# Weight loads on a second issuing engine and a planner that books DMA bandwidth, in an attention and MLP kernel

## The chip, the cores and the metric

The kernel runs on one core of a Trainium2 chip. The metric is the device time of one execution in microseconds (us). Before the change the median of three runs was 182.66 us (180.52 to 183.31). Each run carries a state: "slow" where it took over 1.5% more than the fastest run of the same kernel, "fast" otherwise.

The core has five instruction streams that matter here: TensorE (PE, matrix products), VectorE (DVE), ScalarE (ACT), GpSimd (POOL) and SyncE (SP), which only issues DMA transfers. The profile counts the transfers of all streams on the same 16 DMA engines.

## The reference, cut to what matters

```python
def reference(A_x, A_wqkv, A_wo, B_x, B_w1, B_b1, B_w2, B_b2, c, w_mod):   # x 2048 x 448, F = 1792
    mod = (_silu(c) @ w_mod).reshape(1, 6, 1, -1)
    sa, ca, ga, sb, cb, gb = (mod[:, i] for i in range(6))
    h = _layernorm(x) * (1 + ca) + sa
    x = x + ga * attention(h, wqkv, wo)          # 16 heads of 28, window of 8 keys at stride 2
    h = _layernorm(x) * (1 + cb) + sb
    x = x + gb * mlp(h, w1, b1, w2, b2)          # layernorm, w1, gelu, w2
```

## The kernel before

The kernel does not fix the order of its instructions by hand. Every instruction is a *task* with an engine, an estimated duration and its data. A list scheduler, the planner, simulates the engines. At each moment it gives a free engine the ready task of the highest rank. It repeats this 300 times with noise on the ranks and keeps the best plan (the shortest, with a penalty for gaps in PE's work). The plan fixes only the *order on each engine*. On the chip, an engine waits for data, never for the plan's clock. So if a transfer lands later than the plan assumed, everything behind its first user on that engine waits too.

```python
for e in ("PE", "DVE", "ACT", "POOL", "SP"):
    ...
    for t in ready[e]:
        if ready_at[t] > now or (shared and t.port):
            continue
        key = (t.rank + (SAME if e == "PE" and t.mode_in == mode else 0.0), -t.n)
        ...                                   # the task of the highest key starts now
```

All loads but that of the small vector c are issued from SyncE. Each is one task that is as long as its bytes take at 330 GB/s, so that the plan cannot put two loads at the same time:

```python
def load(fn, nbytes, writes, reads=(), bufs=(), free=False):
    t = add("SP", max(0.5, nbytes / DMA_RATE), fn, writes=writes, reads=reads, bufs=bufs, late=1.8,
            order_after=list(chain_dma))
...
load_k(lambda: wqk_st.t[:, 0], A_wqkv[:, 0:D + HP - DH], "wq", [wqk_st])        # four pieces of Wq and Wk
load_k(lambda: wqk_st.t[:, 1], A_wqkv[:, D:2 * D + HP - DH], "wk", [wqk_st])
...                                                                             # x, Wv, wmod, wo
for kt in range(KT):                                                            # w1: 4 pieces of 448 KB
    load(lambda kt=kt: nc.sync.dma_start(out=w1_s[:, kt], in_=B_w1[KOFF[kt]:KOFF[kt] + 128]), F * 256, [f"w1{kt}"], free=True)
for i in range(4):                                                              # w2: 3 of 448 KB, 1 of 224 KB
    ...
```

Five kinds of small transfer lie on the way from one stage to the next, and they use the same SyncE queue:

```python
add("SP", 1.35, lambda b=b: nc.sync.dma_start_transpose(out=hc.t[...], in_=zs[b].t[:]), ..., late=2.2)     # hT <- z
nc.sync.dma_start(out=v_hbm[r0:r0 + 256]..., in_=vs.t[:]...)                    # v_hbm <- vstage, then
nc.sync.dma_start(out=vb.t[...], in_=src(k0s[0], 2))                            # vb <- v_hbm: keys regrouped
nc.sync.dma_start(out=mod_bc[:], in_=mod_hbm[:]....partition_broadcast(128))    # mod_bc: modulation rows to all partitions
nc.sync.dma_start_transpose(out=yT.t[...], in_=y.t[:])                          # yT <- y, the MLP's input
```

In the order of time the kernel copies Wqk into its packed form on VectorE. It multiplies (`pq`, `pv`), does the attention (`lt`, `pd`, `po`), the output product (`pw`) and the MLP (`p<-yT,w_s`, then `p<-w_s,hm`). All these stages overlap for different blocks of rows. The tile `w_s` in the profile is w1 or w2; z and y are outputs of the layernorms, hT and yT the same transposed, rs_all the reciprocal deviations of the layernorms, oT the output of the attention. The matmul `ptr` transposes z at the start, and `pb` multiplies by wmod. A *gate* below is a small GpSimd task that waits for the Wqk copies.

The softmax here doesn't subtract the row's maximum and nothing guards it: scores larger than these inputs give would overflow.

Of the kernel before, what the change touches and what calls it, by code (L numbers as in the profile page):

```python
# [11 lines left out]
FP32 = mybir.dt.float32  # L12
BF16 = mybir.dt.bfloat16
ACT = mybir.ActivationFunctionType
# [6 lines left out]
HP = 32  # L21
FT = F // 128
# [25 lines left out]
DMA_RATE = 330e3  # L48
SWITCH, SAME = 0.095, 1.0
SEM = 0.07  # L50
DRAIN = {"PE": 0.165, "DVE": 0.085, "ACT": 0.105, "POOL": 0.05, "SP": 0.0}
# [27 lines left out]
class Planner:  # L79
# [68 lines left out]
    def forward(self):  # L148
# [13 lines left out]
        while len(order) < len(self.tasks):  # L162
            started = False
            for e in ("PE", "DVE", "ACT", "POOL", "SP"):
# [115 lines left out]
def kernel(  # L280
# [57 lines left out]
    mod_col = cst.tile([128, 2 * KT], FP32, name="mod_col")  # L338
    mod_half = cst.tile([128, 2 * KT], FP32, name="mod_half")
# [29 lines left out]
    chain_dma = []  # L369

    def load(fn, nbytes, writes, reads=(), bufs=(), free=False):
        t = add("SP", max(0.5, nbytes / DMA_RATE), fn, writes=writes, reads=reads, bufs=bufs, late=1.8,
                order_after=list(chain_dma))
        if not free:
            chain_dma[:] = [t]

    def load_k(dst, src, key, bufs=(), free=False):
        n = src.shape[1]
        for h in range(2):
            load(lambda h=h: nc.sync.dma_start(out=dst()[:, 2 * h:2 * h + 2],  # L380
                                               in_=src[KOFF[2 * h]:KOFF[2 * h] + 256].rearrange("(kt p) n -> p kt n", p=128)),
                 256 * n * 2, [key + "ab"[h]], bufs=bufs, free=free)

    def load_m(dst, col, key, bufs, free=False):
        src = w_mod[:, col:col + 2 * D]
        load(lambda: nc.sync.dma_start(out=dst()[:, 0:2], in_=src[0:256].rearrange("(kt p) n -> p kt n", p=128)),
             512 * D * 2, [key + "a"], bufs=bufs, free=free)
        load(lambda: nc.sync.dma_start(out=dst()[:, 3], in_=src[320:448]), 256 * D * 2, [key + "b"], bufs=bufs, free=free)
        load(lambda: nc.sync.dma_start(out=dst()[64:128, 2], in_=src[256:320]), 128 * D * 2, [key + "c"], bufs=bufs, free=free)

    def fill_m(dst, key, bufs, one, rank):

        def fn():
            nc.gpsimd.memset(dst()[0:64, 2], 0.0)
            if one is not None:
                nc.gpsimd.memset(dst()[0:1, 2, one:one + D], 1.0)

        add("POOL", 1.3, fn, writes=[key + "z"], bufs=bufs, rank_add=rank)

    def load_x(b0, b1):  # L400
        load(lambda: nc.sync.dma_start(out=x_all[:, b0:b1, :], in_=xv[b0 // 8, :, b0 % 8:(b1 - 1) % 8 + 1, :]),
             (b1 - b0) * 128 * D * 2, [f"x{b}" for b in range(b0, b1)], free=b0 >= 8)
# [6 lines left out]
    load_x(0, 2)  # L409
    fill_m(lambda: wm_st.t[:], "wm", [wm_st], D, 850)  # L410
    load_m(lambda: wm_st.t[:], 0, "wm", [wm_st])
    load_k(lambda: wqk_st.t[:, 0], A_wqkv[:, 0:D + HP - DH], "wq", [wqk_st])
    load_k(lambda: wqk_st.t[:, 1], A_wqkv[:, D:2 * D + HP - DH], "wk", [wqk_st])
    load_x(2, 4)
    load_k(lambda: Wv[:], A_wqkv[:, 2 * D:3 * D], "wv")
    load_x(4, 8)
# [7 lines left out]
    load(v_pads, 3 * LEAD * DP * 2, ["v_pads"], reads=["warm_w"], free=True)  # L424
    for i in range(2):
        fill_m(lambda i=i: wmod2[i].t[:], f"wmod2{i}", [wmod2[i]], 0 if i == 1 else None, 300)
        load_m(lambda i=i: wmod2[i].t[:], (2 + 2 * i) * D, f"wmod2{i}", [wmod2[i]], free=True)
    add("POOL", 1.6, lambda: nc.gpsimd.memset(wo_s[:], 0.0), writes=["wo"], rank_add=440)
    wo_v = A_wo.rearrange("(ft r d) n -> r d ft n", r=4, d=DH)
    for r in range(4):  # L430
        load(lambda r=r: nc.sync.dma_start(out=wo_s[HP * r:HP * r + DH, :, :], in_=wo_v[r]), D * D // 2, [f"wo{r}"],
             reads=["wo"], free=True)
    for b in (8, 12):
        load_x(b, b + 4)
    b2_bc = sb("zh", [128, D], BF16, "b2_bc")
    load(lambda: nc.sync.dma_start(out=b2_bc.t[:], in_=B_b2.partition_broadcast(128)), 128 * D * 2, ["b2"], bufs=[b2_bc], free=True)
    load(lambda: nc.sync.dma_start(out=b1_rows[:], in_=B_b1.rearrange("(f p) -> f p", p=128)), F * 2, ["b1_rows"], free=True)
    for kt in range(KT):
        load(lambda kt=kt: nc.sync.dma_start(out=w1_s[:, kt], in_=B_w1[KOFF[kt]:KOFF[kt] + 128]), F * 256, [f"w1{kt}"], free=True)
    for i in range(4):  # L440
        f0, f1 = 4 * i, min(4 * i + 4, FT)
        load(lambda f0=f0, f1=f1: nc.sync.dma_start(
            out=w2_s[:, f0:f1], in_=B_w2[128 * f0:128 * f1].rearrange("(ft p) n -> p ft n", p=128)),
            (f1 - f0) * 256 * D, [f"w2l{f // 2}" for f in range(f0, f1, 2)], free=True)
# [10 lines left out]
    def pool_late():  # L455
        gate = add("POOL", 0.1, lambda: nc.gpsimd.memset(wqk_st.t[0:1, :, KT - 1, 0:8], 0.0), bufs=[wqk_st],
                   writes=["wqb", "wkb"])
        for us, fn, writes, reads, ra in late_pool:
# [6 lines left out]
         ["ident"], gated=False, rank_add=800)  # L465
    pool(0.1, lambda: nc.gpsimd.memset(neg_half[:], -0.5), ["neg_half"])
# [72 lines left out]
    def c_cols():  # L539
        for kt in range(KT):  # L540
            nc.tensor.matmul(psc.t[:, kt:kt + 1], lhsT=c_row[0:1, KOFF[kt]:KOFF[kt] + 128], rhs=one1[:],
                             start=True, stop=True)

    P.wrote(add("PE", 0.2, c_cols, mode="32x128", reads=["c_row", "one1"], bufs=[psc]), psc)
    add("ACT", 0.15, lambda: nc.scalar.activation(out=e_c[:], in_=psc.t[:], func=ACT.Exp, scale=-1.0), bufs=[psc],
        writes=["e_c"], after=[tbl0])
    add("DVE", 0.08, lambda: nc.vector.tensor_copy(out=c_col[:], in_=psc.t[:]), bufs=[psc], writes=["c_col"])
    add("DVE", 0.08, lambda: nc.vector.tensor_scalar_add(out=e_c[:], in0=e_c[:], scalar1=1.0), writes=["e_c"])
    add("DVE", 0.1, lambda: nc.vector.reciprocal(out=e_c[:], in_=e_c[:]), writes=["e_c"])

    def silu():
        nc.vector.tensor_tensor(out=silu_bf[:], in0=e_c[:], in1=c_col[:], op=ALU.mult)
        nc.vector.memset(silu_bf[0:64, 2:3], 0.0)
        nc.vector.memset(silu_bf[0:1, 2:3], 1.0)

    add("DVE", 0.2, silu, reads=["e_c", "c_col"], writes=["silu"])
    pscol = ps_one([128, 2 * KT], "ps_col")

    psmod = ps_one([128, 2 * KT], "ps_mod")

    def mod_cols(dst, kts):
        for v in range(2):
            for j in range(KT):
                for kt in kts:
                    nc.tensor.matmul(dst.t[:, v * KT + j:v * KT + j + 1],
                                     lhsT=wm_st.t[:, kt, v * D + KOFF[j]:v * D + KOFF[j] + 128],
                                     rhs=silu_bf[:, kt:kt + 1], start=(kt == kts[0]), stop=(kt == kts[1]))

    P.wrote(add("PE", 0.5, lambda: mod_cols(pscol, (0, 1)), reads=["silu", "wma"], bufs=[pscol, wm_st]), pscol)
    P.wrote(add("PE", 0.5, lambda: mod_cols(psmod, (3, 2)), reads=["silu", "wmb", "wmc", "wmz"], bufs=[psmod, wm_st]), psmod)  # L570
    add("DVE", 0.08, lambda: nc.vector.tensor_copy(out=mod_half[:], in_=pscol.t[:]), bufs=[pscol], writes=["mod_half"], rank_add=50)
    add("DVE", 0.08, lambda: nc.vector.tensor_tensor(out=mod_col[:], in0=psmod.t[:], in1=mod_half[:], op=ALU.add), bufs=[psmod],
        reads=["mod_half"], writes=["sa", "ca"], rank_add=50)
# [467 lines left out]
```

## Time and profile before

| | before |
|---|---|
| median of three runs | 182.66 us |
| span of the profiled run, granted clock of PE | 182.6 us, 0.981 |
| first projection matmul (`pq`) | 11.83 us |
| first MLP matmul (`p<-yT,w_s`) | 73.62 us |
| from there to the end | 109.0 us |

The profiled run took 184.35 us and is marked slow, about 1% above the median.

The first view cuts the span of the kernel before into stretches. The columns are the stretch (start:end) and its length, then the busy time and number of instructions of PE, PEld (weight load), DVE, ACT and POOL, then the granted clock of PE, the busy share of the DMA engines, and GB/s. Two rows are left out.

```profile
6.00:12.00 6.00, 4.86 (x50) 3.15 (x52) 4.04 (x13) 1.02 (x2) 0.99 (x9) 1.00 1.06 342
12.00:20.00 8.00, 7.54 (x120) 4.56 (x119) 4.85 (x17) 6.05 (x19) 2.39 (x13) 1.00 1.05 281
28.00:36.00 8.00, 7.79 (x185) 3.82 (x186) 4.50 (x14) 7.30 (x15) 1.02 (x1) 1.00 0.48 107
36.00:44.00 8.00, 6.15 (x128) 2.92 (x129) 5.05 (x11) 5.20 (x11) 0.00 (x0) 1.00 0.74 155
44.00:52.00 8.00, 7.90 (x166) 3.68 (x152) 7.09 (x22) 6.84 (x13) 1.41 (x3) 1.00 0.79 231
60.00:68.00 8.00, 7.25 (x104) 3.13 (x105) 6.03 (x19) 7.66 (x16) 2.27 (x4) 1.00 1.02 260
68.00:76.00 8.00, 4.62 (x89) 2.06 (x88) 7.97 (x12) 3.62 (x5) 5.82 (x5) 0.77 0.66 134
76.00:84.00 8.00, 8.00 (x34) 2.84 (x34) 4.83 (x18) 4.59 (x8) 3.16 (x5) 0.80 0.00 1
```

Read the PE column: PE is nearly full from 12 us on, so the kernel is bound by PE work. There are two exceptions. From 36 to 44 us PE works 6.15 of 8 us, and 1.7 us of the rest is a wait for the load of vb. From 68 to 76 us PE works 4.62 of 8 us, and the clock drops behind that hole.

The timeline of the kernel before shows what lies where. Its columns are start, duration, engine (SPq is SyncE's queue of issues), line, operation, output<-input, and the count. In brackets is the idle time before it and what ended that.

```profile
9.79 1.42 DVE L675 COPY Wqk<-wqk_st 128x1024 bf16<-128x1024 bf16 x4
11.83 0.82 PE L585 MATMUL pq<-hT,Wqk 128*128 128x256 bf16 x6
44.47 0.57 SPq L439 DMA_DIRECT2D w_s<-in_B_w_dram  x1
45.56 3.65 SPq L439 DMA_DIRECT2D w_s<-in_B_w_dram  x2
55.91 0.82 SPq L442 DMA_DIRECT2D w_s<-in_B_w_dram  x1
59.13 1.99 SPq L442 DMA_DIRECT2D w_s<-in_B_w_dram  x3
68.21 3.44 SPq L903 DMA_TRANSPOSE yT<-y  x2
```

All four Wqk copies are done in a row at 9.8 us, and `pq` starts right after. The MLP weights leave from 44.5 to 61 us. One transpose of y (54.6 us) leaves among them, and the next three leave behind them, from 63.2 us on.

### The profile page before, as it was taken

The page shows a single profiled execution, that of the slowest core. Times are in us where ns is not written, and L with a number is a line of the kernel's source. Part 1 is how long each engine was busy: PE and PEld are TensorE (multiplying, and loading weights), DVE is VectorE, ACT ScalarE, POOL GpSimd, SP SyncE. Part 2 cuts the span into 40 slices and gives each one's busy share as a digit, 9 for nine tenths or more (in the row PEclk, how much of TensorE's full clock was granted, in tenths as well). Part 3 has the DMA queues.
Part 4 walks back from the last instruction along what each step waited for, and adds up shares of the span by engine and source line. Part 5 has one row for each costly group of instructions (what it writes and reads, how often), then busy time and mean ns, then how long its engine had stood idle before and what let it go on. Part 6 is the DMA issues. An engine that isn't in the chain of part 4 may idle for free.

```text
span 182.6 us, 5017 instructions
## 1 busy us (share of the span) xinstructions
PE 169.1 (93%) x2067; PEld 81.0 (44%) x2085; DVE 115.5 (63%) x318; ACT 107.5 (59%) x195; POOL 49.9 (27%) x83
## 2 busy tenths in 40 slices
PE   7799999959999984899999999999999999999993
PEld 2446654424444532233455534455543344443562
DVE  2577795665999969939634738995569974000121
ACT  3237978876885987147574994762893550644300
POOL 8342022001025608726204005336034533000000
PEclk9999999999999999589999999999999999999999
DMA  5999844595779997300220420025110114001011
GB/s 166 330 342 291 240 122 110 129 176 118 197 258 252 259 233 130 96 0 2 61 57 4 140 79 4 0 57 83 34 50 4 31 29 108 0 4 50 0 50 50
DMA packets 28725, 19.84 MB, mean 109 GB/s; under 512 B 14465, under 2 KB 28062, under 8 KB 28702
## 3 DMA queue, kind: packets, MB, share of 16 engines
q1 hardware_dynamic: 28700, 19.52, 40.8%
q8 instruction: 16, 0.26, 0.7%
q14 instruction: 7, 0.06, 0.1%
q10 hardware_dynamic: 2, 0.00, 0.0%
HBM read 12.41 MB, written 3.96 MB: 90 GB/s over the span
## 4 chain that ended last, share of the span: by engine, by line
PE 82%; DMA 8%; ACT 3%; issue 2%; SPq 2%; DVE 1%; ACTq 0%
PE p L950 24%; PE p L585 22%; PE pq L585 9%; PE pw L877 6%; PE p L591 5%; PE pv L585 5%; DMA wm_st<-in_w_mod_dram 3%; PE lt L796 2%; DMA vb<-v_hbm 2%; PE pq L591 2%; DMA yT<-y 2%; PE po L836 2%; PE pwm L498 1%; PE pv L591 1%; PE pd L828 1%
## 5 line engine op out<-in xcount | busy, mean ns | idle before, releaser
L937 ACT ACTIVATE hm<-p,b_col 128x512 bf16<-128x512 f32 x56 | 35.1, 687 | 32.6 <-PE p L585 17.0
L950 PE MATMUL p<-w_s,hm 128*128 128x448 bf16 (+1 forms) x238 | 44.8, 342 | 0.0
L585 PE MATMUL p<-yT,w_s 128*128 128x512 bf16 x160 | 40.7, 394 | 4.1 <-issue 3.9
L523 POOL TENSOR_TENSOR rs_all<-tv_all,neg_half 128x1 f32<-128x1 f32 (+1 forms) x34 | 22.7, 675 | 59.0 <-DVE tv_all L520 53.4
L950 PEld LDWEIGHTS <-hm 128*128 128x128 bf16 x238 | 22.4, 98 | 18.9 <-issue 0.9
L958 DVE TENSOR_TENSOR x_all<-p,x1p 128x448 bf16<-128x448 f32 (+1 forms) x17 | 10.1, 595 | 29.8 <-PE p L950 29.8
L907 POOL TENSOR_TENSOR x1p<-x_all,gbb_bc 128x448 f32<-128x448 bf16 x16 | 17.6, 1108 | 34.2 <-DVE x_all L958 13.3
L585 PEld LDWEIGHTS <-w_s 128*128 128x128 bf16 x168 | 15.6, 100 | 25.5 <-issue 10.6
L585 PE MATMUL pq<-hT,Wqk 128*128 128x512 bf16 (+1 forms) x111 | 22.9, 334 | 0.9 <-issue 0.6
L806 ACT ACTIVATE et<-lt 128x464 bf16<-128x464 f32 x36 | 17.3, 577 | 8.3 <-PE lt L796 8.2
L505 DVE BATCH_NORM_STATS2 st_all<-x_all 128x6 f32<-128x448 bf16 x32 | 18.9, 612 | 2.5 <-DMA x_all<-in_A_x_dram 2.5
L528 DVE TENSOR_SCALAR z<-x_all,mv,rs_all 128x512 bf16<-128x512 bf16 (+1 forms) x32 | 12.2, 403 | 5.8 <-ACT rs_all L514 3.2
L881 DVE TENSOR_TENSOR x_all<-pw,x_all 128x448 bf16<-128x448 f32 x16 | 9.8, 615 | 9.2 <-PE pw L877 9.2
L814 DVE TENSOR_TENSOR et<-et,mask 128x928 bf16<-128x928 bf16 x18 | 11.6, 665 | 6.1 <-ACT et L806 6.1
L877 PE MATMUL pw<-wo_s,oT 128*128 128x448 bf16 x64 | 14.5, 354 | 0.6 <-DVE oT L862 0.5
L585 PEld LDWEIGHTS <-Wqk 128*128 128x128 bf16 x120 | 10.5, 98 | 9.7 <-issue 2.5
L701 ACT CAST qT<-pq 128x512 bf16<-128x512 f32 (+1 forms) x20 | 9.4, 514 | 6.0 <-PE pq L591 3.9
L862 DVE TENSOR_TENSOR oT<-po,den 128x456 bf16<-128x456 f32 x18 | 10.7, 625 | 2.8 <-ACT den L852 2.8
L701 ACT CAST kT<-pq 128x512 bf16<-128x512 f32 (+1 forms) x20 | 9.0, 515 | 3.2 <-PE pq L585 2.3
L585 PE MATMUL pv<-Wv,hT 128*128 128x448 bf16 x48 | 10.4, 353 | 0.0
L715 ACT CAST vstage<-pv 128x448 bf16<-128x448 f32 x16 | 7.9, 561 | 4.1 <-PE pv L591 3.8
L591 PE MATMUL p<-yT,w_s 64*128 64x512 bf16 x56 | 10.3, 401 | 0.0
(85 smaller groups left out, 172.8 us busy)
## 6 DMA issues: line engine op xcount, KB each, us to landing
w_s<-in_B_w_dram SPq DMA_DIRECT2D x7, 448.0 KB, 4.1
vb<-v_hbm SPq DMA_DIRECT2D x18, 128.0 KB, 2.7
v_hbm<-vstage SPq DMA_DIRECT2D x8, 256.0 KB
out_dram<-x_all SPq DMA_DIRECT2D x7, 224.0 KB, 2.9
x_all<-in_A_x_dram SPq DMA_DIRECT2D x3, 448.0 KB, 5.8
wqk_st<-in_A_wqkv_dram SPq DMA_DIRECT2D x4, 226.0 KB
wmod<-in_w_mod_dram SPq DMA_DIRECT2D x2, 448.0 KB
x_all<-in_A_x_dram SPq DMA_DIRECT2D x2, 224.0 KB
```

The source lines that it names most:

```text
L505: add("DVE", 0.53, lambda: nc.vector.bn_stats(out=st_all[:, sl, :], in_=src()), reads=key, writes=[f"st{sl}"])
L523: lambda: nc.gpsimd.tensor_tensor(out=rs_all[:, which, b0:b0 + n], in0=tv_all[:, which, b0:b0 + n], in1=neg_half[:, 0:n], op=ALU.pow),
L528: return add("DVE", us, lambda: nc.vector.tensor_scalar(out=dst(), in0=src(), scalar1=mv[:, b, 0:1], scalar2=rs_all[:, which, b:b + 1], op ...
L585: nc.tensor.matmul(outs[i].t[:], lhsT=w(i, kt, slice(0, 128)), rhs=x(i, kt, slice(0, 128)), start=(n == 0 and not last), stop=(n == 2 and ...
L591: nc.tensor.matmul(outs[i].t[:], lhsT=w(i, kt, rows), rhs=x(i, kt, rows), start=not last, stop=last, tile_position=(r0, 0))
L701: add("ACT", 0.06 + n / 1200, lambda dst=dst, p=pq[i]: nc.scalar.copy(out=dst, in_=p.t[:]), bufs=[pq[i]], writes=w)
L806: ex = add("ACT", 0.45, lambda r=r: nc.scalar.activation(out=et.t[:, r].rearrange("p n ft c -> p (n ft c)"), in_=lts[r].t[:].rearrange("p ...
L814: nc.vector.tensor_tensor(out=ev, in0=ev, in1=mask[:], op=ALU.mult)
L877: nc.tensor.matmul(pw.t[:], lhsT=oT[:, ft, c0:c0 + 128], rhs=wo_s[:, ft, :], start=(ft == 0), stop=(ft == 3))
L907: P.wrote(add("POOL", 1.05, lambda: nc.gpsimd.tensor_tensor(out=xp.t[:], in0=x_all[:, t, :], in1=gbb2_bc[:], op=ALU.add), reads=[f"x{t}", ...
L937: gl = add("ACT", 0.57, lambda f=f, p=p1[i]: nc.scalar.activation(out=hm_at(f), in_=p.t[:], func=ACT.Gelu_apprx_tanh, bias=b1_col[:, f:f + ...
L950: nc.tensor.matmul(p2.t[:], lhsT=hm_at(f)[:, bi * 128:(bi + 1) * 128], rhs=w2_s[:, f, c0:c1], start=(f == 0), stop=(f == FT - 1))
```

## The change

The intent was to let the weights leave from another engine, so that they no longer stand in SyncE's queue ahead of small urgent transfers. The planner was also to know that bandwidth is shared. Three things were done.

1. Nineteen bulk loads (wmod, wo, x blocks 8 to 15, b2, w1, w2) are issued from GpSimd, each ordered behind the one before it in the plan ("one piece in flight"). That is an ordering edge in the plan, not a wait on the chip.
2. The planner has a sixth engine, BW. Each transfer is a short issue task and a task on BW of its bytes at 340 GB/s. A DMA transpose is booked as 400 KB.
3. The modulation weights are loaded as 4 chunks of 112 rows in place of 128-row pieces, which needs no zero fill.

```diff
-DMA_RATE = 330e3
+DMA_RATE, TR_BYTES = 340e3, 400e3
-            for e in ("PE", "DVE", "ACT", "POOL", "SP"):
+            for e in ("PE", "DVE", "ACT", "POOL", "SP", "BW"):
...
+    def dma(eng, issue, fn, nbytes, writes=(), reads=(), bufs=(), order_after=(), late=1.8, rank_add=0.0):
+        t = add(eng, issue, fn, reads=reads, bufs=bufs, order_after=order_after, rank_add=rank_add, port=None)
+        u = add("BW", nbytes / DMA_RATE, lambda: None, writes=writes, bufs=bufs, order_after=[t], late=late)
+        return t, u
+
+    def head(fn, nbytes, writes, reads=(), bufs=()):
+        t, u = dma("SP", 0.5, fn, nbytes, writes, reads, bufs, list(chain["head"]))
+        chain["head"] = [t]
+
+    def bulk(fn, nbytes, writes, reads=(), bufs=()):
+        t, u = dma("POOL", 0.8, fn, nbytes, writes, reads, bufs, chain["head"] + chain["bulk"], 2.2)
+        chain["bulk"] = [t] + chain["bulkbw"][-1:]
+        chain["bulkbw"].append(u)
...
-        load(lambda kt=kt: nc.sync.dma_start(out=w1_s[:, kt], in_=...), F * 256, [f"w1{kt}"], free=True)
+        bulk(lambda kt=kt: nc.gpsimd.dma_start(out=w1_s[:, kt], in_=...), F * 256, [f"w1{kt}"])
...
-            add("SP", 1.35, lambda b=b: nc.sync.dma_start_transpose(out=hc.t[...], in_=zs[b].t[:]),
-                bufs=[hc, zs[b]], writes=[(hc, "raw", b)], late=2.2)
+            dma("SP", 1.25, lambda b=b: nc.sync.dma_start_transpose(out=hc.t[...], in_=zs[b].t[:]),
+                TR_BYTES, [(hc, "raw", b)], bufs=[hc, zs[b]], late=1.6)
... (the same for wo, x, wmod, yT, v_hbm, vb, mod_bc; the matmuls of the modulation in 112 rows)
```

## The prediction

> **What bounds it now.** The page shows TensorE (PE) busy 93% of a 182.6 us span, and PE is 82% of the chain of waits; the timed median is 182.66 us. The windows view gives PE idle by stage: the first projection matmul (pq) starts at 11.83 us; from 12 to 68 us PE is packed (about 3.4 us idle, 1.7 of it waiting for vb<-v_hbm); from 68 to 74 us PE works only 2.8 of 6 us; after 74 us it idles under 2%. The hole at 68 to 73.6 us ends with a transpose yT<-y that took 4.24 us, on a SyncE (SP) queue that also carried w1 and w2 at 44 to 61 us. After the hole the granted clock is 0.54 from 73.6 to 79.7 us, which I estimate costs 2.6 us (about 15 matmuls took 6.0 us at up to 0.48 us each; at 0.22 they need 3.3). So hole, vb wait and throttle are worth about 9 us; the rest is PE work.
>
> **What moves.** SP drops from 69 to 40 DMA rows; wmod, wo, x blocks 8-15, w1, w2 go to GpSimd (POOL). Three memset pairs of 1.3 us leave POOL; 19 DMA issues come, whose price no trace here shows; the Trainium skill, "DMA: Bandwidth & Descriptors", Latency and other measured facts, has about 1 us to the first byte on this path against 0.6, so I cost them at 1 us each as an estimate. The planner now books bandwidth and 4 us per transpose (booked 2.6, measured 4.0 median for yT).
>
> **Gain.** w1 and w2 leave before the transposes of y, the vb loads no longer queue behind weights, and the order puts 24 pq matmuls, pd/po, pw and pv between the oT that y needs and the first MLP matmul: about 9.9 us of PE work against about 9.2 us for y and its transposes. I expect the hole under 2 us and no throttled stretch behind it, and the vb wait gone: about -8 us.
>
> **Loss, at the start.** "One piece in flight" is only an ordering edge in the plan. The built order shows no wait ahead of the first two wmod pieces (0.8 MB), so they leave at about 3.5 us, while SP still loads wm, Wqk, Wv. The skill says (same page, Queues, rings and completion order) that a DMA engine takes turns between queues; at the 355 GB/s seen here early, that makes Wqk and x 4-7 about 2 us later. VectorE's order also changed: all but one Wqk copy now wait behind mod_half, silu_bc, mod_col, stats of x 2-5 and z 2-3. Adding measured durations (stats 0.6, z 0.4, hT 0.37, Wqk 0.36, silu_bc 0.68), the second copy of the q half ends at about 17 us, 19 with contention. So first pq at 17 to 19 us instead of 11.8, with only the transposes of x 2-3 (0.6 us) done earlier, and part of it at a cold clock although 11 fillers are added: +5 to +7 us.
>
> **Net.** PE has about 54 us of work from first pq to the MLP in both; 18 + 54 + 1 of stalls puts the first MLP matmul near 73 us, as before, but without throttle; the later phases are PE-bound and stay. Predicted 180 us, range 175.5 to 185.5. Faster by over 2%: 0.38; within 2%: 0.53; slower: 0.09.
>
> **Right or wrong in the profile.** wmod packets before 6 us on a POOL queue; first pq after 16 us; no PE idle over 2 us at 65 to 75 us; granted clock near 1 after it; POOL's pow (rs_all) not late.
>
> **What would break it.** GpSimd issues much dearer than 1 us (w1, x 8-15 or rs_all late, a new hole at 35 to 50 us): slower. First pq at 13 us (contention mild, VectorE quicker): 175. A colder start: 183.

## The result, and the profile after

The changed kernel took 192.75 us (median of four runs, 192.24 to 193.26), against 181.87 us of the kernel before in the same rounds. The ratio is 1.0625, 95% interval 1.0536 to 1.0714: slower. Ratios here are the mean time of one kernel's fast runs over that of the other's of the same rounds, so they are not quite the ratio of the medians. The profiled run of the changed kernel was a fast one: span 190.9 us, clock 0.955.

| stage, from the two profiles | before | after | difference |
|---|---|---|---|
| start to first `pq` | 11.83 | 21.84 | +10.0 |
| first `pq` to first MLP matmul | 61.8 | 63.35 | +1.6 |
| first MLP matmul (73.62, 85.19) to the end | 109.0 | 105.7 | -3.3 |

The hole at 68 to 73.6 us lies in the second row, and the half clock behind it in the third. In the second row PE is busy for 55.0 us before and 59.5 us after, with 974 and 973 matmuls, and idle for 6.8 and 3.8 us. So the hole was filled, but PE worked longer on as many matmuls, part of them at a lower clock. The three rows add up to the 8.3 us between the two spans. The medians differ by 10.9, since the profiled run before was a slow one. For that reason the -3.3 is not a clean gain: no fast profile of the kernel before was kept, and in the fast profiles of its close variants (`b1` to `b5` below) the last stretch takes 106.3 to 108.2 us, only 0.6 to 2.5 us more than 105.7.

The same stretches of the changed kernel, in the same columns:

```profile
6.00:12.00 6.00, 6.00 (x60) 3.14 (x58) 0.99 (x5) 0.50 (x2) 0.00 (x0) 1.00 1.08 246
12.00:20.00 8.00, 0.80 (x7) 0.48 (x7) 4.65 (x14) 1.52 (x4) 3.84 (x22) 0.64 0.85 252
20.00:28.00 8.00, 6.64 (x30) 2.94 (x28) 4.04 (x15) 2.92 (x9) 7.23 (x12) 0.50 0.61 189
44.00:52.00 8.00, 4.89 (x149) 2.40 (x148) 7.00 (x14) 3.99 (x8) 1.49 (x1) 0.79 1.06 149
68.00:76.00 8.00, 8.00 (x199) 4.07 (x197) 7.93 (x20) 6.65 (x15) 3.32 (x5) 1.00 0.35 88
```

From 12 to 20 us PE does 0.8 us of work, and from 20 to 28 us it works at half clock. The hole at 68 to 76 us is filled, as predicted. A new one has opened at 44 to 52 us. (PE's 6.00 in the first row is filler that is meant to keep the clock up.)

The timeline of the changed kernel has the answering lines:

```profile
2.87 1.53 POOL L399 DMA_DIRECT2D wmod<-in_w_mod_dram  x2
13.15 0.43 DVE L687 COPY Wqk<-wqk_st 128x1024 bf16<-128x1024 bf16 x1 [5.62 <-DMA wqk_st<-in_A_wqkv_dram]
15.26 0.43 DVE L687 COPY Wqk<-wqk_st 128x1024 bf16<-128x1024 bf16 x1 [1.54 <-DMA wqk_st<-in_A_wqkv_dram]
21.39 0.39 DVE L687 COPY Wqk<-wqk_st 128x1024 bf16<-128x1024 bf16 x1
21.84 1.46 PE L590 MATMUL pq<-hT,Wqk 128*128 128x256 bf16 x6 [1.36 <-DVE Wqk L687]
25.68 1.61 POOL L439 DMA_DIRECT2D w_s<-in_B_w_dram  x3
44.07 0.63 DVE L757 TENSOR_TENSOR wo_s<-wo_s,mod_bc 128x896 bf16<-128x896 bf16 x1 [5.79 <-DMA mod_bc<-mod_hbm]
46.87 0.27 PE L842 MATMUL pd<-et,ones_k 64*32 64x232 bf16 x2 [2.83 <-DVE et L828]
```

Two things went wrong at the start. VectorE waits 5.62 us for the first piece of Wqk. Then the third copy comes only at 21.39 us, six microseconds after the second. In between, VectorE waits for data only once, 0.54 us for x 4 to 7, which took 10.32 us to land. The copy stands behind other VectorE work, because the plan had put it there. The Wqk copies were one group before. In the plan of the change, two of the four Wqk pieces are served on BW only after x 2 to 7 and the first wmod pieces, although SyncE issues them first (planned again from the kernel's source, they start on BW at 10.8 and 13.3 us, and x 2 to 7 at 5.7 and 6.4). BW takes the transfer of the highest *rank*, as the code above shows for every engine, and may let a later issue overtake an earlier one. On the chip the Wqk pieces that VectorE waited for had landed by 15.3 us, and x 4 to 7, issued after them, landed at 18.3 us: no overtaking is seen there.

In the middle, three w1 pieces leave from 25.68 us on, not 44.5. (The fourth leaves at 39.33 us and w2 at 57.1 us, about as before.) They meet a v_hbm store. The chain of work that ended last shows what follows (start, duration, what):

```profile
29.02 6.95 DMA v_hbm<-vstage
38.11 5.83 DMA mod_bc<-mod_hbm
```

SyncE's loads of vb wait for that store until 36.0 us, and the load of mod_bc, whose data were written from 32.6 us on, stands behind them in SyncE's order and leaves at 38.11 us. VectorE waits 5.79 us for mod_bc, and PE waits behind VectorE.

The DMA view from 7 to 11 us shows why the first Wqk piece was late. The first fence is the kernel before, the second the changed one. A queue's line has its packets, megabytes, and the time of its packets as a share of the 16 engines' time; q1 is SyncE's queue and q0 GpSimd's.

```profile
DMA packets 1631, 1.39 MB, mean 348 GB/s; under 512 B 84, under 2 KB 1631, under 8 KB 1631
q1 hardware_dynamic: 1631, 1.39, 106.4%
```

```profile
DMA packets 468, 0.99 MB, mean 248 GB/s; under 512 B 35, under 2 KB 325, under 8 KB 468
q0 software_dynamic: 159, 0.73, 75.3%
q1 hardware_dynamic: 309, 0.26, 32.0%
```

SyncE's queue fell from 348 to 66 GB/s (0.26 MB in 4 us), and the sum of both queues fell as well, to 248. The Trainium skill, "DMA: Bandwidth & Descriptors", section "Queues, rings and completion order", says that a DMA engine takes turns between queues packet by packet. The trace of the changed kernel fits: from 7.5 to 11 us, with both queues at work, it has 149 packets of GpSimd's queue and 200 of SyncE's. It adds the size: SyncE's packets of Wqk are 904 B, one piece of a row each. GpSimd's packets of wmod are up to 5376 B, which is three row pieces of 1792 B. Two queues that take turns by packet do not share by bytes. (The packets are those that the profile counts. `a3`, below, does not fit.)

### The profile page after: what moved, and what is told of

Same layout as the page of the kernel before. It is cut to its first block, busy times and chain, and to the rows that moved or that the text cites. A ratio compares the mean times of both kernels' runs of the same rounds, so it can differ in the third digit from the quotient of the medians.

```text
span 190.9 us, 5058 instructions
## 1 busy us (share of the span) xinstructions
PE 174.1 (91%) x2096; PEld 82.8 (43%) x2096; DVE 116.8 (61%) x317; ACT 108.7 (57%) x195; POOL 59.2 (31%) x99
## 4 chain that ended last, share of the span: by engine, by line
PE 68%; DMA 17%; DVE 10%; SPq 2%; issue 1%; ACT 1%; DVEq 0%
PE p L963 23%; PE p L590 20%; PE pq L590 6%; PE pw L891 5%; DMA x_all<-in_A_x_dram 5%; PE p L596 4%; DMA v_hbm<-vstage 4%; DMA wm_st<-in_w_mod_dram 3%; DMA mod_bc<-mod_hbm 3%; PE pv L590 2%; DVE et L828 2%; PE po L850 2%; PE lt L810 2%; DMA yT<-y 2%; DVE st_all L510 1%; DVE z L533 1%
## 5 line engine op out<-in xcount | busy, mean ns | idle before, releaser
L590 PE MATMUL p<-yT,w_s 128*128 128x512 bf16 x168 | 39.2, 380 | 0.7 <-DMA yT<-y 0.7
L921 POOL TENSOR_TENSOR x1p<-x_all,gbb_bc 128x448 f32<-128x448 bf16 x16 | 17.1, 1071 | 36.5 <-DVE x_all L971 14.2
L590 PE MATMUL pq<-hT,Wqk 128*128 128x512 bf16 (+1 forms) x120 | 26.1, 364 | 1.4 <-DVE Wqk L687 1.4
L590 PEld LDWEIGHTS <-Wqk 128*128 128x128 bf16 x120 | 11.1, 104 | 13.1 <-issue 4.4
L533 DVE TENSOR_SCALAR z<-x_all,mv,rs_all 128x512 bf16<-128x512 bf16 (+1 forms) x32 | 13.4, 439 | 2.0 <-POOL rs_all L528 0.7
L828 DVE TENSOR_TENSOR et<-et,mask 128x928 bf16<-128x928 bf16 x18 | 12.6, 729 | 3.4 <-ACT et L820 3.4
L863 ACT ACTIVATE den<-pd 128x464 f32<-128x464 f32 x18 | 9.3, 584 | 4.4 <-PE pd L842 4.4
L590 PE MATMUL pv<-Wv,hT 128*128 128x448 bf16 x48 | 11.3, 382 | 0.0
```

The source lines that it names most:

```text
L533: return add("DVE", us, lambda: nc.vector.tensor_scalar(out=dst(), in0=src(), scalar1=mv[:, b, 0:1], scalar2=rs_all[:, which, b:b + 1], op ...
L590: nc.tensor.matmul(outs[i].t[:], lhsT=w(i, kt, slice(0, 128)), rhs=x(i, kt, slice(0, 128)), start=(n == 0 and not last), stop=(n == 2 and ...
L828: nc.vector.tensor_tensor(out=ev, in0=ev, in1=mask[:], op=ALU.mult)
L921: P.wrote(add("POOL", 1.05, lambda: nc.gpsimd.tensor_tensor(out=xp.t[:], in0=x_all[:, t, :], in1=gbb2_bc[:], op=ALU.add), reads=[f"x{t}", ...
```

## The experiments

Eighteen kernels ran, all with correct results. The overview gives the ratio to the kernel before of the same rounds; "pq" and "MLP" are the first projection and first MLP matmul.

| run | edit | median us | ratio (95%) | pq | MLP |
|---|---|---|---|---|---|
| after | the change | 192.75 | 1.0625 (1.054, 1.071) | 21.84 | 85.19 |
| a5 | after, other seed | 194.29 | 1.0629 (1.049, 1.077) | 17.24 | 84.01 |
| a2 | after, bulk from SyncE | 190.99 | 1.0511 (1.035, 1.067) | 17.58 | 83.77 |
| a3 | after, two wmod pieces from ScalarE | 189.43 | 1.0444 (1.035, 1.054) | 21.29 | 82.57 |
| a1 | after, two wmod pieces behind a gate | 190.35 | 1.0502 (1.044, 1.057) | 16.55 | 83.04 |
| a7 | a1, scaling of wo later | 191.04 | 1.0522 (1.039, 1.065) | 18.14 | 83.97 |
| a8 | a1, two in flight for real | 196.33 | two fast runs | 17.11 | 88.29 |
| a14 | a1, w1 and w2 held | 191.66 | two fast runs | 16.55 | 82.44 |
| a6 | in-order BW in the plan, gate | 188.64 | 1.0373 (1.027, 1.047) | 11.14 | 78.69 |
| a9 | a6, two in flight for real | 193.25 | 1.0672 (1.058, 1.077) | 10.55 | 86.44 |
| a13 | a6, w1 and w2 held | 184.05 | 1.0196 (1.011, 1.029) | 10.59 | 78.78 |
| a11 | in-order BW, bulk from SyncE | 186.77 | 1.0353 (1.027, 1.044) | 11.19 | 78.89 |
| a12 | a11, w1 and w2 held | 183.55 | 1.0170 (1.009, 1.025) | 10.47 | 75.24 |
| a15 | a12, plan at 300 GB/s | 179.13 | 0.9874 (0.980, 0.995) | 10.39 | 72.00 |
| b1 | before, other seed | 183.12 | 1.0092 (0.999, 1.019) | | |
| b2 | before, transposes of y booked longer | 183.88 | 1.0136 (1.004, 1.022) | | |
| b3 | before, 112-row chunks | 182.28 | 1.0039 (0.995, 1.013) | | |
| b4 | before, w1 and w2 early | 186.88 | 1.0393 (1.032, 1.046) | 11.26 | 76.67 |
| b5 | before, last w2 pieces 6 us earlier | 181.01 | 0.9986 (0.993, 1.004) | 11.37 | 72.98 |

### The first round: engine, order, chunks or luck

The first theory was that GpSimd's early wmod packets starve SyncE (theory 1, or T1). The rivals were the plan's order, the chunks, and the random draw of the plan. `a1` moves the first two wmod issues behind a GpSimd task that waits for the Wqk copies, and keeps the rest of the order:

```diff
     P.plan()
+    early = chain["issued"][:2]
+    rest = [x for x in P.order if x[0] not in early]
+    k = [t for t, _ in rest].index(chain["gate"]) + 1
+    P.order = rest[:k] + [x for x in P.order if x[0] in early] + rest[k:]
     P.emit()
```

> The changed kernel, in its own planned order, with the first two pieces of the modulation weights (0.8 MB) moved behind the GpSimd memset that waits for the Wqk copies, so that they cannot leave before the head loads have landed. Theory T1 (these two pieces, in software packets of 5.4 KB against the 0.9 KB packets of the head loads, starve the SyncE queue from 7 to 11.5 us): SyncE's queue keeps about 340 GB/s through 7 to 11 us instead of 66, the first Wqk copy starts near 9.5 us instead of 13.2, the first pq matmul at 16 to 17.5 us instead of 21.8, and the time falls by 4 to 6 us to 187 to 189 us. Rival T2 (the new order on VectorE and TensorE alone makes the start late, the two pieces only take their share of bytes): first pq stays above 20 us and the time within 1.5 us of 192.7.

`a2` issues every bulk load from SyncE (`nc.gpsimd.dma_start` becomes `nc.sync.dma_start` in those 19 places), with the order of the plan kept:

> The changed kernel, in its own planned order, with all 19 bulk loads issued from SyncE instead of GpSimd: one queue, first in first out, so nothing overtakes the head loads. T1 (sharing between the two queues is what hurts): first pq at 16 to 17.5 us, the first v_hbm store lands in under 4 us instead of 7, and the time is 183 to 188 us. T2 (the plan's order): 190 us or more. A third possibility, T3 (SyncE issues too slowly[...], which is what the change meant to cure): the start is good but vb loads and transposes are late, a hole opens before the first MLP matmul, and the time is 189 to 193.

`a3` issues the two wmod pieces from ScalarE, at about 6.6 us, whose queue made packets of 1792 B:

```diff
-        load_m(bulk, nc.gpsimd, ...)
+        load_m(bulk, nc.gpsimd if i else nc.scalar, ...)     # and moved in ScalarE's order behind the first rs_all
```

> The changed kernel, in its own planned order, with only the first two modulation pieces issued from ScalarE (a second hardware queue, 1.8 KB packets) right behind its first rstd pair, at about 6.6 us, so that their packets start within 1 us of when the software ones did (6.9 us). If packet size sets the shares (T1), the SyncE queue keeps a third to a half of the bytes instead of a quarter, its 7 to 11 us rate is 110 to 170 GB/s instead of 66, the first pq comes at 18.5 to 20.5 us and the time falls by 1 to 3 us. If any second stream of 0.8 MB costs the same (rival), the first pq stays within 0.7 us of 21.8 and the time within 1 us of the changed kernel.

In `a1` SyncE's queue was back at about 349 GB/s from 7 to 11 us, and the first two Wqk copies came at 8.51 and 9.86 us. The first `pq` came at 16.55 us. So the starvation is real and costs 5.3 us of the start. The remaining 4.7 us are VectorE's order: the third Wqk copy was still at 16.10 us. But of those 5.3 us only about 2.4 reached the end, because VectorE now waited 8.5 us for mod_bc. So `a1` missed the time of its theory (187 to 189 us). `a2` has no GpSimd DMA at all and is still 1.0511, in the ranges of its rivals T2 and T3. Its `pq` comes at 17.58 us.

In `a3` the packets were 904 B against 1792 B, and from 7 to 11 us the two queues moved 217 and 103 GB/s. That mean hides a change: ScalarE's packets start only at about 9.3 us, so the first Wqk copies came early, at 8.89 and 10.67 us. From 10 to 12 us, with Wv and x 4 to 7 still to land, the DMA view has (q10 is ScalarE's queue)

```profile
q10 hardware_dynamic: 299, 0.51, 104.5%
q1 hardware_dynamic: 11, 0.01, 2.2%
```

SyncE was starved more than beside GpSimd, by packets only twice the size of its own. So the size of the packets alone does not set the shares, and turns by packet do not come out of this run; why stays open. VectorE then waited 3.5 us for x 4 to 7, ahead of the third Wqk copy in its order, and `pq` stayed at 21.29 us, within the rival's 0.7 us. The time fell by 3.3 us, outside the ranges of both. The starvation by a second queue is shown, by `a1`; packet size as its reason is not. Of the whole loss the issuing engine is the smaller part (`a2`), and the order of the plan the larger.

`b3` took the chunks alone into the kernel before (the loads, the zero fills and the matmuls of the change, with the old planner):

> The kernel before with only the modulation part of the change: 112-row chunks, no memset pairs on GpSimd, the ones row added as a bias, and planned again by the old planner, all loads on SyncE. I expect 180 to 185 us, that is the same as before within the luck of a plan; if the chunks themselves cost (112 of 128 partitions, four rows of DRAM per partition), wm_st lands over 1 us later than 7.5 us and first pq over 1 us later than 11.8 us.

They are neutral (1.0039, with an interval around 1). `b1` and `a5` change only the seed of the planner's noise, 7 to 8:

> The kernel before with only its planner's random seed changed from 7 to 8. It measures how far a new plan moves the time with no other change: if luck of the plan could be the cause of the 11 us, it lies more than 4 us from 182; I expect within 3 us of it, 179.5 to 185.5.

> The changed kernel with another random seed of its planner, nothing else. If the loss is the change's (theory 1: any order that this planner makes has the rank-served bandwidth and the same packets): 189 to 196 us, first pq after 16 us. Rival (the order of seed 7 is an unlucky draw): within 2 per cent of the kernel before, under 186.

A new draw moved the kernel before by 0.9% with an interval that reaches 1.0, and the changed kernel not at all (1.0629, from two fast runs). As far as two draws of each can say, the loss is not bad luck. `b2` books the transposes of y 1.4 us longer in the plan before (`late=1.3` becomes `late=2.7`), as the change does:

> The kernel before with one number changed: its planner books 4.0 us from issue to landing for each yT transpose (1.3 + 2.7) instead of 2.6, and plans again. If the wrong latency in the plan made the hole at 68 to 73.6 us, the new order has less than 3 us of TensorE idle between 65 and 76 us and the time falls by 2 to 5 us to 177 to 180. If a new plan moves the time by luck whatever is booked, it falls or rises by up to 3 us and the hole may stay.

The hole stayed (1.06 us of PE work from 68 to 74 us), so booking the transposes longer does not fill it by itself.

`a7` was a miss. It starts from `a1` and moves VectorE's scaling of wo, the work that waits for mod_bc, behind the first two attention divisions:

```diff
+    late = [x for x in P.order if x[0] in chain["wos"]]
+    rest = [x for x in P.order if x[0] not in chain["wos"]]
+    k = max(i for i, (t, _) in enumerate(rest) if t in chain["div"][:2]) + 1
+    P.order = rest[:k] + late + rest[k:]
```

> The kernel of the run a1 with one more move in its order: VectorE's two scalings of wo_s, which wait for mod_bc, stand behind the first attention block's divisions instead of ahead of its masks. In a1 VectorE sat for mod_bc until 41.2 us and the first pd matmul came at 44.0. If this wait is what gives the start's gain back, the first pd comes at 36 to 39 us, the first MLP matmul at 78 to 81 instead of 83.0, and the time is 185 to 188 us instead of 190.4. If the middle is bound elsewhere (VectorE's total work, DMA landings of x 8-15, vb), the first MLP matmul stays within 1 us and the time within 1 us of a1.

The wait moved, it did not go: VectorE now waited 6.1 us for transposes hT<-z, and PE 4.3 us behind it. That was the first sign that the middle is late not for one transfer but for whichever one is due there.

### The plan's bandwidth engine

`a6` makes BW serve in order of issue, orders the first bulk load behind the gate, and drops the pacing edges:

```diff
                     key = (t.rank + (SAME if e == "PE" and t.mode_in == mode else 0.0), -t.n)
+                    if e == "BW":
+                        key = (-ready_at[t], -t.n)
...
-        chain["bulk"] = [t] + chain["bulkbw"][-1:]
+        chain["bulk"] = [t]
+        chain.setdefault("issued", []).append(t)
...
+        P._edge(gate, chain["issued"][0], False)
```

> The changed kernel planned again with two corrections: the plan's bandwidth engine serves transfers in order of issue instead of by rank, and the first bulk load is ordered behind the GpSimd memset that waits for the Wqk copies (so in the built program it really waits). Built, its VectorE order has all four Wqk copies ahead of the statistics of x 2-3, as the kernel before has. If the wrong service order in the plan made the late start (T4), first pq comes at 10.5 to 13 us and the time falls to 180 to 186 us. If the plan's order is not what costs (rival: GpSimd's traffic beside SyncE's through the middle), the start is good and the time stays above 188.

The first `pq` came at 11.14 us, earlier than in the kernel before. Gate and in-order service together take the start back, and `a1` shows that the gate alone does not. (`a11`, below, has in-order service without the gate and without a second queue, and its `pq` comes at 11.19 us, against 17.58 us in `a2` with service by rank. All of these are new plans.) Yet the time stayed at 1.0373, because the middle was worse. In the timeline of `a6`:

```profile
22.18 2.13 POOL L442 DMA_DIRECT2D w_s<-in_B_w_dram  x4
22.65 1.81 SPq L800 DMA_DIRECT2D vb<-v_hbm  x2
33.90 0.68 PE L854 MATMUL po<-et,vb 64*32 64x57 bf16 x64 [2.15 <-DMA vb<-v_hbm]
```

The load of vb was issued at 22.65 us and its last half landed at 33.86, beside all eight w1 and w2 pieces. The v_hbm store behind it took 12.5 us, and PE later waited 4.2 us for the scaling of wo that needs mod_bc.

### Real pacing

If too many bulk pieces at once are the trouble, the pacing should be real. `a9` (from `a6`, pacing edges kept) and `a8` (from `a1`) let GpSimd read one element of piece k before it issues piece k+2:

```diff
+        def go():
+            if k >= 2:
+                nc.gpsimd.tensor_copy(out=seen[0:1, k:k + 1], in_=landed[k - 2]())
+            fn()
```

> The kernel of the run with the in-order bandwidth plan (188.64 us), with the pacing edges back in the plan and made real: before GpSimd issues bulk piece k+2 it copies one element of piece k, so at most two bulk pieces are in flight. Theory 1 (what is left of the loss, once the plan orders the Wqk copies early, is SyncE's small packets starved by many bulk pieces at once): first pq near 11 us, the vb<-v_hbm load under 5 us instead of 10.4, the v_hbm store under 4 us, time 181 to 185. Rival (pacing makes GpSimd stand in waits, so x 8-15, rs_all or the weights come late, and the order stays longer for other reasons): vb short, but new waits on the bulk tiles, time 187 or more.

> The run with the first two modulation-weight pieces behind the gate (190.35 us), its order kept, with real pacing: GpSimd copies one element of bulk piece k before it issues piece k+2. Theory 1 (starvation costs the middle part, the plan's order the start): first pq stays at 16 to 17.5 us, v_hbm store under 4 us, mod_bc under 5 us instead of 6.9, time 186.5 to 189.5. Rival (the middle is late from the order on VectorE and TensorE alone): v_hbm and mod_bc shorter, but time 190 to 192.

Both were misses and much slower (`a8`: the mean of its two fast runs over that of the fast runs before is 1.078). The rival for `a9` held, in its number and its kind. The view of waits of `a9` (engine, line, waited for: total us, times, longest) has it on PE, then on VectorE:

```profile
PE lt L827 <- POOL kT L493: 7.6, 1, 7.6
DVE et L845 <- POOL mask L505: 9.5, 1, 9.5
```

GpSimd does its tasks in order. While it stands waiting for a weight piece, the small fills of kT and the mask behind it wait too, and PE and VectorE wait for those. In `a8` it was GpSimd's rs_all that VectorE waited for (4.7 us), and PE 8.6 us behind it. An engine that also computes is a poor place for a wait on DMA.

### Early weights

By now every version had a hole between 24 and 52 us, at a different transfer each time. What they had in common was the moment at which w1 and w2 left: 22 to 30 us in `a6`, from 25.7 us in the changed kernel (three pieces of eight), 44.5 to 61 us before. `a11` still had them early, with no DMA on GpSimd (the edits of `a2` on the plan of `a6`):

> The in-order bandwidth plan with all bulk loads issued from SyncE, no DMA on GpSimd. Theory 1 (two causes: the plan serves bandwidth by rank though the queue is in order, and GpSimd's large packets starve SyncE's small ones; this kernel has neither): first pq near 11 to 12 us, vb<-v_hbm under 6 us, no hole before the first MLP matmul, time 178 to 185. Rival (the plan's order is bad for another reason, or the weights ahead in the one queue hold up vb and mod_bc): first pq early but waits over 3 us for vb, mod_bc or y's transposes in the middle, time 187 or more.

It came out at 1.0353, the same as `a6` within their intervals. The rival was right: first `pq` at 11.19 us, then VectorE waited 6.5 us for transposes of h, issued from 31.5 us on (before: from 27.4) behind the weights in the one queue, and PE worked 4.87 of 8 us from 44 to 52 us, at a clock of 0.56. So the engine that issues is not the question; when the weights go is.

Theory 3 said so: w1 and w2 at 19 to 33 us meet the transposes of h, the v_hbm store, vb and mod_bc. The rival, theory 5, was that the new order on VectorE and TensorE is late in itself. Four runs bear on it. `a12` and `a13` are planned anew, so their order on the compute engines is new too; `a14` and `b4` keep it. `a12` and `a13` hold w1 and w2 behind mod_bc, on SyncE and on GpSimd:

```diff
+        for t in chain["issued"][-8:]:            # a12: behind the issue of mod_bc's load
+            P._edge(mt, t, False)
...
+        P._edge(gt, chain["issued"][-8], False)   # a13: behind GpSimd's product of b2 and the gate
```

> The run with the in-order bandwidth plan and bulk on SyncE (186.77 us), with w1 and w2 held behind the load of mod_bc in the plan and so on SyncE's queue. Theory 3 (early weights meet the latency-bound transfers of the middle): first pq near 11 us, no PE wait over 2 us from 24 to 52 us, time 180 to 184. Theory 5 (the order on the compute engines is late in itself): holes of 3 us or more stay in the middle, 186 or more.

> The run with the in-order bandwidth plan and bulk on GpSimd (188.64 us), with w1 and w2 placed behind GpSimd's product of b2 and the gate, which needs mod_bc, so that they leave after about 35 us. Theory 3: vb<-v_hbm under 4 us instead of 10.4, time 181 to 185. Theory 5: vb shorter, but new waits of VectorE's order, 186.5 or more.

> The run with the first modulation pieces behind the gate (190.35 us), its order on every other engine kept, with w1 and w2 issued by GpSimd only behind its product of b2 and the gate. Theory 3: v_hbm store and mod_bc under 4.5 us (mod_bc was 6.9), first pd before 41 us, time 185.5 to 188; first pq stays near 16.5. Theory 5: transfers shorter, time 189.5 to 191.

`b4` is the opposite edit, in the kernel before, with every other order kept:

```diff
     P.plan()
+    early = issued[-8:]                           # w1 and w2
+    rest = [x for x in P.order if x[0] not in early]
+    k = [t for t, _ in rest].index(max(wo_done, key=lambda t: t.start)) + 1
+    P.order = rest[:k] + [x for x in P.order if x[0] in early] + rest[k:]
     P.emit()
```

> The kernel before, its order kept, with the eight w1 and w2 loads moved on SyncE's queue directly behind the last wo piece, so that they leave at about 27 us instead of 44 to 61. Theory 3: the transposes of h and vb between 28 and 42 us take 4 us and more, PE idles 3 us or more there, the hole at 68 us shrinks under 2 us, and the time is 183 to 188. Theory 5 (early weights cost little): 182.5 or less, perhaps faster than before because the hole at 68 us is gone.

`b4` lost 3.9%, with nothing changed but the place of eight issues. The first fence has its timeline, the second its chain of work that ended last (start, duration, what):

```profile
27.19 4.48 SPq L445 DMA_DIRECT2D w_s<-in_B_w_dram  x4
39.31 0.41 DVE L531 TENSOR_SCALAR z<-x_all,mv,rs_all 128x512 bf16<-128x512 bf16 x1 [9.23 <-DMA hT<-z]
40.31 0.76 PE L799 MATMUL lt<-qT,kT 28*64 28x58 bf16 x61 [7.63 <-DVE oT L865]
```

```profile
29.05 2.62 SPq L445
31.71 1.10 SPq L785
32.91 6.37 DMA hT<-z
39.31 0.03 DVE z L531
```

Follow the chain from the top. The eight issues, from 25.34 us on, keep SyncE until 31.67 us; the last took 2.62 us, the seven before it 0.38 to 0.67 us each. So the first transpose of h was issued at 32.91 us and not at 27.35 as before, and its data, behind the weights in the queue, took 6.37 us (the median of the six transposes from 25 to 45 us is 2.6 us). VectorE waited 9.23 us for that transpose to release its input buffer, and PE 7.63 us behind VectorE. And the hole at 68 us went, just as in the changed kernel: PE worked 8.00 of 8 us from 68 to 76 us. `b4` pays for its weights some 35 us earlier than the kernel before, and more.

`a12` and `a13` gained 1.8 points each from holding the weights, on either engine (from 1.0353 to 1.0170, from 1.0373 to 1.0196). Both are inside theory 3's range and below theory 5's. What seems to remain in `a13` is the sharing of queues. GpSimd's weights leave at 34 to 39 us there, and the DMA view of `a13` from 39 to 46 us, with the transposes still in flight, reads

```profile
q0 software_dynamic: 414, 1.97, 83.4%
q1 hardware_dynamic: 308, 0.17, 9.8%
```

In the kernel before the eight transposes hT<-z of this stretch took 2.4 us from issue to landing (median of 25 to 55 us); in `a13` it is 11.6 us. The two lines are from the DMA view, the kernel before first:

```profile
hT<-z SPq DMA_TRANSPOSE x8, 2.4
```

```profile
hT<-z SPq DMA_TRANSPOSE x8, 11.6
```

The packets of the two queues differ again: mostly 256 B for a transpose, up to 7168 B for a weight. VectorE waited 5.50 us and PE 7.88 us. The profiled run of `a13` was a slow one, so this needs a fast run beside it: `a14`, below, is one, and its median there is 11.7 us.

`a14` missed its range. It holds the weights in the changed kernel's own order, and they then left at 35.6 us, in the middle of four transposes of h issued at 34.3 us. VectorE waited 6.2 us for those, PE 7.1 us. Against `a1`, with only the eight issues moved, the middle did improve: the v_hbm store of 8.6 us took 3.3 us, mod_bc left at 28.86 us in place of 34.22 and took 5.1 us in place of 6.9, and the first `pd` came at 37.5 us in place of 44.0. But the collision only changed its victim. The mean of its two fast runs is 1.053 of that of the fast runs before. It fits neither theory as written: holding helps only where the weights then find a gap.

### What was left

`a12` was still 1.7% behind, with PE waiting 1.6 us for normalized x blocks (z, ahead of `ptr`) and 1.5 us for wmod before 21 us, and half clock from 20 to 28 us. The plan believes in 340 GB/s there. The trace showed 333 GB/s from 6 to 12 us and 256 from 12 to 20. `a15` books 300 (`DMA_RATE` 340e3 becomes 300e3) and replans:

> The run with the in-order plan, bulk on SyncE and w1/w2 held (183.55 us), with the plan's bandwidth booked at 300 instead of 340 GB/s. If the plan's too early landings are what is left: PE waits for ptr and pb before 24 us shrink from 1.6 and 1.5 us to under 1 us, no half clock from 20 to 28 us, time 179 to 182. Rival (the rest is the draw of the plan, about 1 per cent either way): waits of the same size elsewhere, 182.5 to 186.

```profile
12.00:20.00 8.00, 7.54 (x121) 4.63 (x119) 6.26 (x19) 6.62 (x21) 2.44 (x12) 1.00 1.08 244
20.00:28.00 8.00, 7.85 (x71) 3.86 (x69) 7.05 (x22) 5.92 (x15) 1.03 (x1) 1.00 0.81 224
68.00:76.00 8.00, 8.00 (x42) 3.45 (x41) 8.00 (x23) 5.56 (x9) 3.06 (x4) 1.00 0.46 84
```

These are the windows of `a15`: the start is full, the clock is 1.00, and the hole is gone. The time is 179.13 us, ratio 0.9874 (0.980 to 0.995): below the kernel before throughout the interval, though by less than 2%. The stated waits went. But all of `a15`'s order is a new draw, its first w1 pieces left at 44.1 us in place of 28.8 in `a12`, and a draw alone can be worth about 1%. How much of the 3 points from `a12` is the rate is open.

`b5` tried the hole of the kernel before directly, moving its last four w2 issues to 50.2 us, with the rest kept (the same kind of edit as `b4`):

> The kernel before with its last four w2 loads moved on SyncE's queue from 56 to 61 us to directly behind the fourth w piece at 52.5 us, everything else kept. If the hole at 68 to 73.6 us comes from w2 beside the transposes of y: VectorE's 1.9 us wait for w2 goes, the yT load is under 3 us, the hole shrinks by 2 us or more, 178 to 180.5. Rival (the v_hbm store, vb and the first yT, now behind the weights, are later by as much): PE waits 2 us or more at 55 to 64 us, 181 to 185.

The ratio is 0.9986: no gain. VectorE's wait for w2 went, but PE waited 1.8 us for yT instead and still worked only 6.11 of 8 us from 68 to 76 us. The chain of work has the rival's reason: a v_hbm store at 53.19 us, right behind the moved weights, took 7.74 us, and the work up to that transpose of y hangs on it. Again the weights met another transfer.

## Why the prediction was wrong, point by point

**Right.** The first wmod pieces were issued early (2.87 us), though their packets came at 6.86 us and not before 6. The first `pq` came after 16 us. VectorE's order had moved the Wqk copies back. The hole at 68 to 73.6 us went, and the clock behind it was 1.00. GpSimd's issues were not dear: 0.54 to 0.84 us each for the weights and up to 1.17 us for x, against the 1 us assumed.

**Wrong: "about 2 us later" and so "+5 to +7 us" for the start.** It was +10.0 us. The prediction had the mechanism, queues taking turns, but shared by time as if packets were alike. SyncE, with 904 B against up to 5376 B, got 66 GB/s, not half of 355, and the sum fell too. (After `a3` the size of the packets can be only part of the reason.) `a1` measured this term at 5.3 us. Then PE, idle for 7.2 us, started `pq` at half clock: 1.46 us for six matmuls that took 0.82 us before. The Trainium skill, "TensorE: Matmul & The Clock Gate", part 1, says that the clock falls to half after an idle window of about 3.4 us and comes back after at least one busy window of that length. The fall agrees: the clock was 0.50 when `pq` started. It came back at about 28 us, after 6.1 us of full PE work. The prediction said "part of it at a cold clock", but gave it no number of its own.

**Wrong: "18 + 54 + 1 of stalls puts the first MLP matmul near 73 us".** It came at 85.19 us, 12.2 us later, and each term failed. The 18 was 21.84 us. The 54 of work was 59.5 us of busy PE, where the kernel before took 55.0 us for as many matmuls. The lower clock explains the difference: as an estimate from the windows, about 3.0 us are lost right behind the cold start (6.16 us at a clock of 0.51) and about 1.7 us behind the hole at 44 us (0.72 from 46 to 52 us). The 1 of stalls was 3.8 us, of which 3.1 us are PE's wait for VectorE, behind mod_bc. So by the profile the late start and its cold clock make up about 6.9 of the 12.2 us. But repairing the start alone did not bring that back: `a6` has its first `pq` at 11.14 us and is still 3.7% behind.

What the prediction missed in the middle is this. It counted "w1 and w2 leave before the transposes of y" as pure gain. It never asked what they would meet instead. w1 and w2 are 3.44 MB, which is about 9.8 us of the whole DMA path at 350 GB/s (an estimate from the measured rate), and that block has to lie somewhere. Before, it lay at 44 to 66 us. The change moved its front to 25.7 us, onto the v_hbm store (6.95 us), and mod_bc came late behind that store; with no weights beside it mod_bc still takes 4.5 us (`a13`) or 5.1 us (`a14`). In the changed kernel's own order `a14` shows this mechanism, but not its price, since its time did not fall. `b4` shows a price with nothing else changed, 3.9%, in the kernel before; `a12` and `a13` gain 1.8 points by holding the weights, with new plans. The prediction did list "a new hole at 35 to 50 us" among what would break it, but as a result of dear issues, which they were not.

**Wrong in size: "about -8 us" of gain.** The hole went, but the part after the first MLP matmul gained 3.3 us at most (see the table), and the prediction's 2.6 us for the half clock was read from a slow run. Of the 11 runs of the kernel before in the last round, two had a granted clock of 1.00 (179.40 and 180.04 us) and the others 0.979 to 0.991; the profiled one had 0.981. The fast profiles of `b3` and `b5` still have the hole, but a clock of 1.00 behind it, so part of the expected gain was not there to be had in every run.

**Also wrong: the pacing.** The prediction saw that "one piece in flight" is only an edge in the plan. It did not ask whether making it real would help. `a8` and `a9` say that on GpSimd it would not.

**The ledger.** From the changed kernel at 1.0625: the gate for two pieces brings it to 1.0502 (`a1`); in-order service of BW, with a gate, to 1.0373 (`a6`); SyncE as the issuer to 1.0353 (`a11`), no real difference; holding the weights to 1.0170 (`a12`); the lower rate, or the new draw with it, to 0.9874 (`a15`). From `a6` on each step is also a new plan, so a point of any of them may be the draw. The change's idea, to plan bandwidth, may be worth about 1% once the plan behaves like the queue (`a15`), which is also what a draw can be worth. Its other idea, a second issuing engine, shows no gain: each pair that differs mainly in the issuing engine (after and `a2`, `a6` and `a11`, `a13` and `a12`) differs by about 1.1 points at most. The Trainium skill, "DMA: Bandwidth & Descriptors", section "Issuing engines are not separate DMA queues", says as much: transfers run on the same 16 engines whichever engine starts them.

What stays open is how much of `a15` is the rate and how much the draw, why the hole of the kernel before stays in `b2`, and what sets the shares of two queues, since `after` fits turns by packet and `a3` does not.

## What to carry to other kernels

A bulk load that is moved away from one critical transfer will lie on another: before moving it, list what is due in the stretch where it lands, and put it where the DMA share is low and nothing short and urgent is in flight. Keep bulk transfers of another queue away from small ones that someone waits for: the share that is left to them can be far from half (66 of 248 GB/s here, and 11 packets beside 299). A planner that models a resource should serve it as the traces show it served (here in order of issue, at the measured rate), or it will order its instructions around landings that come later than planned.

## What the Trainium skill lacked or had wrong

- "DMA: Bandwidth & Descriptors", "Queues, rings and completion order", has the turns by packet, but not what follows for two queues with packets of different size. Here 904 B beside 5376 B left 66 of 248 GB/s to the small ones, and 256 B transposes beside weights of up to 7168 B had 9.8% of the engines' time against 83.4%, and took 11.6 us in place of 2.4 (a slow run; 11.7 us in the fast `a14`). In `a3` turns by packet do not come out, if packets are what the profile counts: 11 packets of SyncE passed beside 299 of 1792 B.
- The same page, "SWDGE vs HWDGE vs iDMA", gives a packet as "≤4096 B preferably". The packets of GpSimd's queue here were up to 5376 and 7168 B, three and two row pieces, while SyncE's and ScalarE's held one row piece each (904 and 1792 B).
- The same page, "Rules for kernel authors", says that spreading transfers over several engines for bandwidth doesn't help. Here it could also hurt: the sum fell from 348 to 248 GB/s from 7 to 11 us. The same table says that a transpose next to ordinary DMAs needs nothing. That is about correctness, and the results agree; its time was another matter (the 11.6 us above).
- The same page, "Latency and other measured facts", gives about 1 us to the first byte for a transfer issued from GpSimd. From the start of the issue to the first wmod packets it was 4.0 us here (2.87 to 6.86 us), with two issues of together 1.53 us in between and SyncE's queue keeping the engines full.
- No page that was used here gives the cost of an issue on GpSimd by itself: 0.54 to 0.84 us here for weights of 98 to 448 KB.
